# Routed attention and mixture of experts in one kernel: sums two pairs back and similarities moved to the head of a pair, routing a pair later

## The chip, the cores and the metric

The kernel runs on one core of a Trainium2 chip. The core has a matmul engine (PE, with its weight loads shown as PEld), a vector engine (DVE), a scalar engine for activations and copies (ACT), a general engine (POOL) and an engine that issues transfers (SP). [...] they wait for each other by semaphores. The metric is the device time of one execution in microseconds (us); less is better.

## The reference

Two blocks follow each other. The first is attention with routing: every query and every key is assigned to the nearest of 16 centroids of its head, and a query attends only to keys of its own cluster. The second sends every row of the result, 3072 rows of 512 numbers, to one of eight experts. Cut to what matters:

```python
# q, k, v: (4, 8, 768, 64); centroids: (8, 16, 64)
q_assign = argmax(einsum('bhsd,hcd->bhsc', q_n, c_n), -1)   # normalised
k_assign = argmax(einsum('bhsd,hcd->bhsc', k_n, c_n), -1)
mask = q_assign[..., :, None] == k_assign[..., None, :]
scores = where(mask, q @ k.T / 8, -1e9)
attn = softmax(scores)
x = (attn @ v).transpose(0, 2, 1, 3).reshape(3072, 512)

logits = x @ w_gate                     # (3072, 8)
e = argmax(logits, 1)
gate_w = softmax(logits)[row, e]
y[row] = gate_w * (relu(x[row] @ w1[e]) @ w2[e])
```

## The kernel before, in words

**Pairs.** There are 4 sequences (`B`) of 8 heads. The attention works on two heads at a time; the loop over `n` runs over 16 such pairs, four to a sequence (`HP` is 4). A pair has two halves `h` of 384 queries each, and six blocks `j` of 128 keys. For each of the 12 combinations `score` (L426 to L433) puts the products of keys and queries into a score tile `sps` and adds a mask product of 16-bit one-hot rows, `mk` and `mq`, to it; ACT then takes the exponential into a tile `A` (L445). There are three score tiles and twelve `A` tiles. From the second block of a half on, `add_up` (L451, DVE) adds the `A` tiles into `acc`. After all 12, `attend` (L457) multiplies the values by the `A` tiles, first for half 0, then for half 1, and ACT copies each finished half into `oT` (L464).

**What hangs around this stream.** Each step is a small function, placed by hand at a slot (`at_pair(n, u, f)`): `between(n, u)` runs the list of slot `u` of pair `n` in the order in which it was filled. Slots 0 to 5 lie behind the six scores of half 0 and their adds, 6 to 11 behind those of half 1, 12 behind the attention outputs of half 0, and 13 at the end of the pair.

- *For the next pair.* `prepare(n, step)`: step 0 (`turn`, L277) transposes the queries and keys just loaded; step 1 (`similar`, L291) multiplies them by the centroids on PE into a bank `mps`; steps 2 and 3 (`assign0`, `assign1`, `assign2`, L302 to L327) find on DVE each row's cluster and end with the one-hot transpose `ohT`; steps 4 and 5 (`place`, L337 and L340) copy it on ACT into `mk` and `mq`, in eight operations, keys first.
- *For the pair before.* `sum_up` (L480) sums the columns of `acc` on PE and multiplies `oT` by the gate weights, 24 matmuls into another bank `mps`; `weights_of` (L489 to L504) takes the reciprocals of the sums and collects the logits on DVE; `rows` (L510, DVE) transposes `oT`, and `store` (L517, SP) writes it to memory in four transfers.
- *Routing of a finished sequence b.* `gate`, `gate_exp` (ACT), `gate_sum` and `choose` make the softmax weight and the choice of expert; `count` (L592, L593, two small matmuls) and `number` (L598 to L605) give each row its place in its expert's list, which six indirect transfers on POOL write (L607). `count` writes into free columns of the bank that the latest `sum_up` took.

The similarities, the sums and the two halves of the attention output share two banks of the pool `ps_m`; a new tile takes a bank whose former contents have been read. In a pair the sums come first, then the similarities, then the two halves.

**Order around the change.** `sum_up` of pair n-1 and `similar` of pair n+1 stand at slot 2, so PE does three scores, sums, similarities, and then the other nine scores. `weights_of` stands at slot 2 too, `rows` and `store` at 4, the two parts of the assignment at 5 and 7, `place` at 11, and the transposes of pair n+2 behind slot 12. The transfers of queries, keys and values of pair n+2 are issued on SP at the beginning of pair n.

**Late in the attention.** In pair 12 sequence 2 is complete. Its routing is done faster, since two first expert slots are filled from sequences 0 to 2 while pairs 13 to 15 still run: `number` in pair 13, then `rank_first` (L645 to L650), places, gathers. The expert stages follow (L968, L1069 and L1088 are their matmuls); at their start the last pair's sums and the routing of sequence 3 are done.

Of the kernel before, what the change touches and what calls it, by code (L numbers as in the profile page):

```python
# [33 lines left out]
def kernel(  # L34
# [12 lines left out]
    B, H, S, D = q.shape  # L47
# [8 lines left out]
    HP = H // 2  # L56
    NPAIR = B * HP
# [28 lines left out]
    wa = ctx.enter_context(tc.tile_pool(name="weights_a", bufs=1))  # L86
    w1s = ctx.enter_context(tc.tile_pool(name="w1_sums", bufs=1))
    xp = ctx.enter_context(tc.tile_pool(name="rows", bufs=1))
    accp = ctx.enter_context(tc.tile_pool(name="accp", bufs=3))
    otp = ctx.enter_context(tc.tile_pool(name="otp", bufs=2))  # L90
    stat = ctx.enter_context(tc.tile_pool(name="stat", bufs=2))
    rt = ctx.enter_context(tc.tile_pool(name="route", bufs=1))
# [75 lines left out]
    with tc.manual_schedule(), ExitStack() as actx:  # L168
# [12 lines left out]
        def load(n):  # L181
            b, hp = divmod(n, HP)
            for d, src, name in ((QIN, q, "q_in"), (KIN, k, "k_in")):
                t = d[n] = ld.tile([P, NI, Q4], F32, name=name)
                for r in range(4):
                    s = src[b, 2 * hp + r // 2, :, Q4 * (r % 2) : Q4 * (r % 2 + 1)]
                    nc.sync.dma_start(
                        out=t[Q4 * r : Q4 * (r + 1)].rearrange("t (j a) d -> t j a d", a=4),
                        in_=s.rearrange("(a t j) d -> t j a d", a=4, j=NQ),
                    )  # L190
            if n:
                load_v(n)

        def load_v(n):
            b, hp = divmod(n, HP)
            VIN[n] = ldv.tile([P, 2, NQ, D], F32, name="v_in")
            for a in range(2):
                nc.sync.dma_start(
                    out=VIN[n][:, a], in_=v[b, 2 * hp + a].rearrange("(p j) d -> p j d", j=NQ)
                )  # L200
# [73 lines left out]
        def turn(n, w):  # L274
            src, dst, name = ((QIN, QT, "qT"), (KIN, KT, "kT"))[w]
            dst[n] = qkt.tile([P, S], F32, name=name)
            nc.vector.transpose(dst[n], src.pop(n).rearrange("p i d -> p (i d)"))  # L277
# [9 lines left out]
        def similar(n):  # L287
            ps = ps_m.tile([P, 512], F32, name="mps")
            for g in range(4):
                t = (QT, KT)[g // 2][n]  # L290
                nc.tensor.matmul(  # L291
                    ps[Q4 * g : Q4 * (g + 1), 0:HS],
                    lhsT=cT[:, n % HP].rearrange("p a c -> p (a c)"),
                    rhs=t[:, HS * (g % 2) : HS * (g % 2 + 1)],
                    start=True, stop=True,
                )
            SIM[n] = ps

        def assign0(n, part=1):

            sim = asg.tile([P, HI, 2 * C], F32, name="sim")[:, 0 : HI // part]
            nc.vector.transpose(sim.rearrange("p i c -> p (i c)"), SIM.pop(n)[:, 0 : HS // part])  # L302
            SIM[n] = sim.rearrange("p i (a c) -> p (i a) c", c=C)

        def assign1(n, part=1):
            G = 2 * HI // part
            sim = SIM[n]
            mx = asg.tile([P, 2 * HI], F32, name="mx")[:, 0:G]
            nc.vector.tensor_reduce(mx, sim, axis=AX, op=ALU.max)
            ge = asg.tile([P, 2 * HI, C], BF16, name="ge")[:, 0:G]  # L310
            nc.vector.tensor_tensor(ge, sim, mx.unsqueeze(2).to_broadcast([P, G, C]), op=ALU.is_ge)
            SIM[n] = ge

        def assign2(n, part=1):
            G = 2 * HI // part
            ge = SIM.pop(n)
            rank = asg.tile([P, 2 * HI, C], BF16, name="rank")[:, 0:G]
            nc.vector.tensor_tensor(rank, ge, first_cb[:, None, :].to_broadcast([P, G, C]), op=ALU.mult)
            top = asg.tile([P, 2 * HI], BF16, name="top")[:, 0:G]
            nc.vector.tensor_reduce(top, rank, axis=AX, op=ALU.max)  # L320
            oh = asg.tile([P, HI, 2 * C], BF16, name="oh")[:, 0 : HI // part]
            nc.vector.tensor_tensor(
                oh.rearrange("p i (a c) -> p (i a) c", c=C), rank, top.unsqueeze(2).to_broadcast([P, G, C]),
                op=ALU.is_equal,
            )
            OH[n] = asg.tile([P, HS], BF16, name="ohT")[:, 0 : HS // part]
            nc.vector.transpose(OH[n], oh.rearrange("p i c -> p (i c)"))  # L327

        def place(n, w):
            t, m = OH[n], (MQ, MK)[w][n % 2]  # L330
            for h in range(2):
                for a in range(2):
                    g = 2 * w + h
                    dst = m[D * a : D * a + Q4, HS * h : HS * (h + 1)]
                    src = t[Q4 * g : Q4 * (g + 1), :]
                    if w == 0:
                        nc.scalar.copy(dst, src)  # L337
                    else:
                        big, less = (t[Q4 * g : Q4 * (g + 1), a : a + 1] for t in (ksc2, kscn2))
                        nc.scalar.activation(dst, src, AF.Identity, bias=less, scale=big)  # L340
            if w == 0:
                OH.pop(n)
# [95 lines left out]
        def score(n, h, j):  # L438

            if n + h or j > 2:  # L440
                score_half(n, h, j, True)
            score_half(n, h, j, False)
            ps = SP.pop((n, h, j))
            A[n, h, j] = ap.tile([P, 2, HS], F32, name="A")
            nc.scalar.activation(A[n, h, j], ps[:, :, 0:HS], AF.Exp, scale=D**-0.5)  # L445

        def add_up(n, h, j):
            if j == 1:
                ACC[n, h] = accp.tile([P, 2, HS], F32, name="acc")
            first = A[n, h, 0] if j == 1 else ACC[n, h]  # L450
            nc.vector.tensor_tensor(ACC[n, h], first, A[n, h, j], op=ALU.add)  # L451
# [70 lines left out]
        def prepare(n, step):  # L522
            if not 0 <= n < NPAIR:
                return
            if step == 0:
                turn(n, 0)
                turn(n, 1)
            elif step == 1:
                similar(n)
            elif step == 2:  # L530
                assign0(n)
                assign1(n)
            elif step == 3:
                assign2(n)
            elif step == 4:
                place(n, 1)
            else:
                place(n, 0)
# [285 lines left out]
        def at_pair(n, u, f, *a):  # L824
            AT.setdefault((n, u), []).append(lambda: f(*a))

        for n in range(NPAIR):
            if n:
                at_pair(n, 2, sum_up, n - 1)
                at_pair(n, 4, rows, n - 1)  # L830
                at_pair(n, 4, store, n - 1)
            for u, step in ((2 if n else 6, 1), (5 if n else 7, 2), (7 if n else 8, 3), (11, 4), (11, 5)):
                at_pair(n, u, prepare, n + 1, step)
        for b in range(B - 1):
            n = HP * (b + 1)
            last = b == B - 2
            at_pair(n, 5 if last else 10, gate, b)
            at_pair(n, 8 if last else 11, gate_exp, b)
            at_pair(n + (not last), 9 if last else 3, gate_sum, b)
            at_pair(n + (not last), 10 if last else 9, choose, b)  # L840
            at_pair(n + 2 - last, 2, count, b)
            at_pair(n + 2 - last, 3 if last else 6, number, b)
        for n in range(1, NPAIR):
            at_pair(n, 2, weights_of, n - 1)
        n = HP * (B - 1)
        slots = range(len(EARLY))
        at_pair(n + 1, 4, rank_first)
# [20 lines left out]
        def between(n, u):  # L868
            for f in AT.pop((n, u), ()):
                f()  # L870
# [4 lines left out]
        for n in range(NPAIR):  # L875
            if n + 2 < NPAIR:
                load(n + 2)
            for h in range(2):
                for j in range(NQ):
                    score(n, h, j)  # L880
                    if j:
                        add_up(n, h, j)
                    between(n, h * NQ + j)
            for h in range(2):
                for j in range(NQ):
                    attend(n, h, j)
                if h == 0:
                    between(n, 12)
                    prepare(n + 2, 0)
            between(n, 13)  # L890
        assert not AT

# [1 line left out]
    with tc.manual_schedule(), ExitStack() as ectx:  # L894
# [262 lines left out]
        n = NPAIR  # L1157
        last = NS - 1
# [9 lines left out]
        for s in range(NS):  # L1168
# [26 lines left out]
            if s < last:  # L1195
# [16 lines left out]
                if s == 0:  # L1212
                    when = ((h2, 1), (h2, 2), (h2, 5), (h2, 6), (h2, 7), (h2, 7))
                elif s == 1:
                    when = ((h1, 9), (h1, 12), (h2, 2), (h2, 3), (h2, 6), (h2, 6))
                else:
                    when = ((h1, 9), (h1, 10), (h2, 1), (h2, 2), (h2, 2), (h2, 5))
# [297 lines left out]
```

## Time and profile before

| | |
|---|---|
| runs of the kernel | 660.87 us median of 3 (659.3 to 662.08) |
| the profiled execution | 659.27 us |
| its span in the profile | 657.5 us |
| PE busy | 644.2 us (98%) |
| DVE busy | 490.0 us (75%) |
| ACT busy | 338.8 us (52%) |
| POOL busy | 130.8 us (20%) |
| attention pairs 1 to 15 | 31.8 to 329.5 us of the span |
| exponentials L445, each | 814 ns, 192 of them |
| adds L451, each | 948 ns, 128 of them |
| copies of outputs L464, each | 481 ns, 32 of them |
| ACT waiting for `ohT` before `place` | 39.7 us in 15 waits |

The span runs from the first to the last instruction of the profile; 1.8 us of the execution lie around it. Busy time of PE is modelled for the ends of its matmuls, so the starts of its instructions are read for its rhythm, not the sum of its busy time. A line such as `150.39 0.92 PE L433 ...` in the timeline gives the start, the length, the engine, the line of the kernel and the tiles; brackets at its end give the idle time before it and what ended it. In a table of stages each row is a stretch of the span, with its length and the busy time of every engine in it, and the number of instructions in parentheses.

### The profile page before, as it was taken

To read this page: it belongs to the slowest core of one execution; us is meant where nothing else is said; L and a number is where in the kernel's file an instruction comes from. 1 tells how busy PE (TensorE), PEld (TensorE's weight loads), DVE (VectorE), ACT (ScalarE), POOL (GpSimd) and SP (SyncE) were. 2 spreads that over 40 slices of the span, in tenths; PEclk is the share of its full clock that TensorE was granted. 3 is DMA by queue.
4 is the path that set the end of the run, shared out by engine and by line. 5 is a ranking of instruction groups with operands and counts; after the bars stand their busy time and mean duration, and the time that the engine had idled before them with its cause. 6 is when DMAs were issued, how large, how long until landed. Compare 5 with 4: busy or idle time off the path is not lost.

```text
span 657.5 us, 11491 instructions
## 1 busy us (share of the span) xinstructions
PE 644.2 (98%) x4252; PEld 423.3 (64%) x4252; DVE 490.0 (75%) x845; ACT 338.8 (52%) x584; POOL 130.8 (20%) x166
## 2 busy tenths in 40 slices
PE   8999999999999999999999999999999999999996
PEld 4444544455444454544484979989797987869773
DVE  6988888998889988989887997888869365572300
ACT  4677878768878777867532333333231331323210
POOL 4500000022000300041103522324240422140010
PEclk9999999999999999999999999999999999999999
DMA  7663455443355433347475587776684835614010
GB/s 150 150 120 68 76 94 97 72 80 68 73 97 98 74 76 72 72 132 227 117 273 156 187 314 264 252 275 211 249 307 170 273 138 165 233 74 173 7 49 19
DMA packets 189760, 95.38 MB, mean 145 GB/s; under 512 B 152895, under 2 KB 171839, under 8 KB 188416
## 3 DMA queue, kind: packets, MB, share of 16 engines
q1 hardware_dynamic: 184624, 81.56, 45.2%
q0 software_dynamic: 4928, 12.97, 6.1%
q8 instruction: 35, 0.57, 0.4%
q14 instruction: 29, 0.24, 0.1%
q10 hardware_dynamic: 144, 0.03, 0.0%
HBM read 74.10 MB, written 20.70 MB: 144 GB/s over the span
## 4 chain that ended last, share of the span: by engine, by line
PE 80%; issue 10%; DVE 5%; POOL 2%; ACT 1%; DMA 1%; POOLq 0%; DVEq 0%; ACTq 0%
PE sps L433 20%; PE mps L457 16%; PE bank L968 10%; PE sbank L968 8%; PE bank L1069 7%; PE bank L1088 7%; PE sbank L1069 6%; PE mps L480 2%; PE mps L291 1%; PE bank L937 1%; DMA xg<-x_rows,gi 1%; DVE xT L780 1%; POOL tokens_of L607 1%; DVE acc L451 1%; DVE a L789 1%
## 5 line engine op out<-in xcount | busy, mean ns | idle before, releaser
L445 ACT ACTIVATE A<-sps 128x768 f32<-128x768 f32 x192 | 152.1, 814 | 30.0 <-PE sps L433 29.4
L433 PE MATMUL sps<-qT,kT 64*128 64x384 f32 x768 | 158.9, 492 | 0.0
L451 DVE TENSOR_TENSOR acc<-acc,A 128x768 f32<-128x768 f32 x128 | 121.4, 948 | 11.4 <-ACT A L445 2.9
L457 PE MATMUL mps<-A,v_in 128*64 128x384 f32 x768 | 127.4, 488 | 0.0
L433 PEld LDWEIGHTS sps<-qT,kT 64*128 64x128 f32 x768 | 66.8, 187 | 52.2 <-issue 48.4
L457 PEld LDWEIGHTS mps<-A,v_in 128*64 128x64 f32 x768 | 53.7, 137 | 70.6 <-issue 62.9
L1043 POOL DMA_INDIRECT out_dram<-z,si x30 | 47.7, 1590 | 196.0 <-DVE z L926 167.2
L607 POOL DMA_INDIRECT tokens_of<-tg,pos_i x24 | 27.5, 1147 | 270.5 <-DVE pos_i L605 264.4
L433 PE MATMUL sps<-mq,mk 64*128 64x384 bf16 x384 | 64.9, 323 | 3.1 <-ACT mq L337 1.3
L1088 PE MATMUL bank<-w,h 128*128 128x512 f32 (+2 forms) x224 | 64.4, 596 | 0.0
L340 ACT ACTIVATE mk<-ohT,kscn,ksc 32x384 bf16<-32x384 bf16 x60 | 42.0, 700 | 40.5 <-DVE ohT L327 39.7
L968 PE MATMUL bank<-xT,w 128*128 128x144 f32 (+4 forms) x288 | 47.7, 309 | 0.0
L738 POOL DMA_INDIRECT xg<-x_rows,gi x30 | 38.4, 1280 | 47.0 <-DVE si L729 16.4
L968 PE MATMUL sbank<-xc,a 128*128 128x144 f32 (+4 forms) x288 | 47.7, 309 | 0.0
L1088 PEld LDWEIGHTS bank<-w,h 128*128 128x128 f32 (+2 forms) x224 | 24.6, 151 | 32.5 <-issue 32.3
L968 PEld LDWEIGHTS bank<-xT,w 128*128 128x128 f32 x288 | 43.8, 190 | 2.6 <-issue 2.2
L451 DVE TENSOR_TENSOR acc<-A 128x768 f32<-128x768 f32 x32 | 30.4, 952 | 19.2 <-ACT A L445 19.1
L968 PEld LDWEIGHTS sbank<-xc,a 128*128 128x128 f32 x288 | 43.4, 190 | 0.0
L926 DVE TENSOR_TENSOR h<-sbank,p 128x288 f32<-128x288 f32 (+4 forms) x18 | 9.2, 514 | 45.7 <-PE sbank L968 45.5
L433 PEld LDWEIGHTS <-mk 64*128 64x128 bf16 x384 | 19.9, 94 | 29.0 <-DVE mk L383 2.6
L986 ACT ACTIVATE h<-h 128x288 f32<-128x288 f32 (+4 forms) x36 | 17.6, 488 | 38.1 <-DVE h L926 38.1
L755 DVE TENSOR_TENSOR xw<-xg,sf 128x256 f32<-128x256 f32 (+2 forms) x60 | 32.8, 606 | 0.9 <-DMA xg<-x_rows,gi 0.6
(216 smaller groups left out, 900.5 us busy)
## 6 DMA issues: line engine op xcount, KB each, us to landing
w<-in_moe_w_dram SPq DMA_DIRECT2D x20, 2048.0 KB, 10.7
v_in<-in_v_dram SPq DMA_DIRECT2D x32, 192.0 KB, 2.5
x_rows<-x SPq DMA_DIRECT2D x64, 96.0 KB, 2.4
turn_rows<-xw SPq DMA_DIRECT2D x23, 256.0 KB, 2.0
q_in<-in_q_dram SPq DMA_DIRECT2D x60, 96.0 KB, 3.2
k_in<-in_k_dram SPq DMA_DIRECT2D x60, 96.0 KB, 3.2
xs<-turn_rows SPq DMA_DIRECT2D x16, 144.0 KB, 2.8
xs<-turn_rows SPq DMA_DIRECT2D x8, 208.0 KB, 4.2
```

Source lines behind the costliest of these rows:

```text
L340: nc.scalar.activation(dst, src, AF.Identity, bias=less, scale=big)
L433: nc.tensor.matmul(SP[n, h, j][:, a, 0:HS], lhsT=kt[rows, j * P : (j + 1) * P], rhs=qt[rows, h * HS : (h + 1) * HS], start=first, stop=not ...
L445: nc.scalar.activation(A[n, h, j], ps[:, :, 0:HS], AF.Exp, scale=D**-0.5)
L451: nc.vector.tensor_tensor(ACC[n, h], first, A[n, h, j], op=ALU.add)
L457: nc.tensor.matmul(O[n, h][D * a : D * (a + 1), 0:HS], lhsT=VIN[n][:, a, j, :], rhs=A[n, h, j][:, a, :], start=(j == 0), stop=(j == NQ - 1),)
L607: ins = nc.gpsimd.indirect_dma_start(out=t_d[:, :], out_offset=bass.IndirectOffsetOnAxis(ap=pos_i[:, i : i + 1], axis=0), in_=tg[:, b, i, ...
L738: nc.gpsimd.indirect_dma_start(out=xg[0:m], out_offset=None, in_=x_d[0:rows_in, :], in_offset=bass.IndirectOffsetOnAxis(ap=g["gi"][0:m, j ...
L755: nc.vector.tensor_tensor(xw[0:m, :, :, d2 * a : d2 * (a + 1)], xg[0:m].rearrange("p (r a d b) -> p a r b d", r=HP, a=2, b=DB)[:, a], g["s ...
L968: nc.tensor.matmul(ps[:, f * T2 : (f + 1) * T2], lhsT=w[:, k, (2 * j + f) * P : (2 * j + f + 1) * P], rhs=x[:, k, :], start=first and f + ...
L1043: ins = nc.gpsimd.indirect_dma_start(out=out[:, :], out_offset=bass.IndirectOffsetOnAxis(ap=GR[s]["si"][0:rows, j : j + 1], axis=0), in_=z ...
L1069: nc.tensor.matmul(ps[:, 0:H], lhsT=x[:, k, :], rhs=y[:, k, :], start=first and k == 0, stop=k == 3, skip_group_check=not first,)
L1088: nc.tensor.matmul(ps[i * m : (i + 1) * m, :], lhsT=h[:, f, j * P : j * P + m], rhs=w[:, f, :], start=(k == 0), stop=(k == FB // n - 1),)
```

## The change

Up to pair 11 the sums of a pair are made two pairs later instead of one, at a new slot -1 ahead of the first score, and the similarities of the next pair stand beside them:

- for pairs 2 to 12 slot -1 runs `sum_up(n-2)`, slot 0 `weights_of(n-2)`, slot 3 `rows` and `store` of pair n-2 (in pair 12 these at slot 0);
- from pair 12 on `sum_up(n-1)` stays at slot 2, and `weights_of` goes to slot 3, `rows` and `store` to 5 in pair 12 and stay at 4 after it; pair 12 so has the sums of pairs 10 and 11;
- for pairs 2 to 11 `similar` goes to slot -1, the assignment to slots 2 and 4, and the transposes of pair n+2 from behind slot 12 to slot 9; elsewhere they stay;
- the routing of sequences 0 and 1 is one pair later: `gate` at slot 10 of pair 4b+5, `gate_exp` at slot 13, and so on; that of sequence 2 stays;
- `acc` has four buffers instead of three.

```diff
-    accp = ctx.enter_context(tc.tile_pool(name="accp", bufs=3))
+    accp = ctx.enter_context(tc.tile_pool(name="accp", bufs=4))
...
+        LATE = HP * (B - 1)
+
+        def pair_end(n, u, v, m):
+            at_pair(n, u, sum_up, m)
+            at_pair(n, u + 1, weights_of, m)
+            at_pair(n, v, rows, m)
+            at_pair(n, v, store, m)
+
         for n in range(NPAIR):
-            if n:
-                at_pair(n, 2, sum_up, n - 1)
-                at_pair(n, 4, rows, n - 1)
-                at_pair(n, 4, store, n - 1)
-            for u, step in ((2 if n else 6, 1), (5 if n else 7, 2), (7 if n else 8, 3), (11, 4), (11, 5)):
-                at_pair(n, u, prepare, n + 1, step)
+            if n >= 2 and n <= LATE:
+                pair_end(n, -1, 3 if n < LATE else 0, n - 2)
+            if n >= LATE:
+                pair_end(n, 2, 5 if n == LATE else 4, n - 1)
+            if n == 0:
+                steps = (6, 7, 8, 11, 11, 12)
+            elif n == 1 or n >= LATE:
+                steps = (2, 5, 7, 11, 11, 12)
+            else:
+                steps = (-1, 2, 4, 11, 11, 9)
+            for step, u in enumerate(steps):
+                at_pair(n, u, prepare, n + 1 + (step == 5), (step + 1) % 6)
         for b in range(B - 1):
             n = HP * (b + 1)
             last = b == B - 2
-            at_pair(n, 5 if last else 10, gate, b)
-            at_pair(n, 8 if last else 11, gate_exp, b)
-            at_pair(n + (not last), 9 if last else 3, gate_sum, b)
-            at_pair(n + (not last), 10 if last else 9, choose, b)
-            at_pair(n + 2 - last, 2, count, b)
-            at_pair(n + 2 - last, 3 if last else 6, number, b)
-        for n in range(1, NPAIR):
-            at_pair(n, 2, weights_of, n - 1)
+            if last:
+                when = ((n, 5), (n, 8), (n, 9), (n, 10), (n + 1, 2), (n + 1, 3))
+            else:
+                when = ((n + 1, 10), (n + 1, 13), (n + 2, 3), (n + 2, 9), (n + 3, 2), (n + 3, 6))
+            for (m, u), f in zip(when, (gate, gate_exp, gate_sum, choose, count, number)):
+                at_pair(m, u, f, b)
...
         for n in range(NPAIR):
             if n + 2 < NPAIR:
                 load(n + 2)
+            between(n, -1)
             for h in range(2):
...
                 if h == 0:
                     between(n, 12)
-                    prepare(n + 2, 0)
             between(n, 13)
```

## The prediction

> **What bounds the kernel now.** I read the page first (TensorE 98% busy, chain of waits 80% PE), then stage by stage. Below, busy time by stage, one row for each pair of heads: the stretch, its length, then busy time by engine.
>
> ```profile
> core 0: us, PE busy (x) PEld busy (x) DVE busy (x) ACT busy (x) POOL busy (x), PEclk, DMA share, GB/s
> 31.80:51.55 19.75, 19.75 (x154) 9.66 (x153) 16.68 (x25) 15.93 (x25) 0.00 (x0) 1.00 0.71 122
> 130.51:150.39 19.88, 19.88 (x157) 9.78 (x155) 18.30 (x32) 14.55 (x22) 5.28 (x5) 1.00 0.43 79
> 150.39:170.13 19.74, 19.74 (x155) 9.66 (x153) 17.36 (x27) 15.77 (x25) 1.98 (x2) 1.00 0.43 79
> 249.22:268.96 19.74, 19.74 (x154) 9.68 (x152) 16.95 (x35) 14.94 (x23) 0.00 (x0) 1.00 0.47 86
> 268.96:288.84 19.88, 19.88 (x156) 9.77 (x154) 18.21 (x45) 11.90 (x18) 6.77 (x6) 1.00 0.21 45
> 288.84:310.37 21.53, 20.21 (x154) 9.89 (x152) 19.49 (x37) 17.47 (x27) 4.58 (x4) 1.00 0.76 254
> ```
>
> A pair takes 19.74 us, or 19.88 where `count` falls into it (pairs 6, 10, 13), and PE is busy through all of it; DVE has 1.6 to 3.1 us free, ACT 3.8 or more. Only pair 14 is longer: 21.53 us, 1.3 of it idle. The chain of waits has the same rhythm:
>
> ```profile
> 43.73 7.89 PE mps L457 x48
> 51.62 2.62 PE sps L433 x18
> 54.24 1.11 PE mps L480 x24
> 56.00 7.47 PE sps L433 x54
> ```
>
> Three scores 2.62, sums 1.11, similarities 0.65 (what is left to 56.00), nine scores 7.47, attention outputs 7.89: 19.74. So up to pair 13 a pair costs what PE's own stream costs, and a moved step earns only what it changes in that stream. The timeline of PE shows what that can be (start, length):
>
> ```profile
> 150.39 0.92 PE L433 MATMUL sps<-qT,kT 64*128 64x384 f32 x4
> ...
> 151.30 0.81 PE L433 MATMUL sps<-qT,kT 64*128 64x384 f32 x4
> ...
> 152.11 0.81 PE L433 MATMUL sps<-qT,kT 64*128 64x384 f32 x4
> ...
> 153.01 0.86 PE L480 MATMUL mps<-acc,ones_s 128*32 128x192 f32 x16
> ...
> 154.01 0.49 PE L291 MATMUL mps<-qT,cT 128*32 128x384 f32 x2
> ...
> 154.77 0.92 PE L433 MATMUL sps<-qT,kT 64*128 64x384 f32 x4
> ...
> 155.68 0.81 PE L433 MATMUL sps<-qT,kT 64*128 64x384 f32 x4
> ```
>
> A score follows a score after 0.81 us (0.807 on average). It takes 0.91 (150.39 to 151.30) as the first after the outputs, 0.90 as the last before the sums, 0.91 after the similarities (154.77 to 155.68), and 0.90 before the outputs. Each change of matmul kind costs about 0.1. The outputs alone, 24 times 0.3225 (start to start of their weight loads), are 7.74, so 7.89 holds 0.05 of their start and 0.10 at their end. The same 7.89 lies between the last outputs (321.58) and the full-width matmul after them (329.47), so that 0.10 isn't the scores' doing.
>
> The one stall, and the work around a head on ACT:
>
> ```profile
> 290.86 0.32 PE L433 MATMUL sps<-mq,mk 64*128 64x384 bf16 x1 [1.10 <-ACT mq L337]
> 291.39 0.32 PE L433 MATMUL sps<-mq,mk 64*128 64x384 bf16 x1 [0.21 <-ACT mq L337]
> ```
> ```profile
> 151.54 0.86 ACT L464 COPY oT<-mps 128x384 f32<-128x384 f32 x2
> 152.28 2.24 ACT L445 ACTIVATE A<-sps 128x768 f32<-128x768 f32 x3
> 155.94 7.21 ACT L445 ACTIVATE A<-sps 128x768 f32<-128x768 f32 x9 [1.43 <-PE sps L433]
> 165.52 2.85 ACT L340 ACTIVATE mk<-ohT,kscn,ksc 32x384 bf16<-32x384 bf16 x4 [2.36 <-DVE ohT L327]
> ```
>
> The mask matmul of pair 14 needs the fifth and sixth of eight `place` operations. `place` waits for the one-hot transpose `ohT` on DVE, and the copies of the outputs (L464) stand behind `place` on ACT: in pair 6 they run from 151.54 to 152.40, up to 2.0 us after the head of pair 7 at 150.39.
>
> [...] 0.1 us at each change (scores 64x128, outputs 128x64, sums 128x32). [...] the L464 copy of pair 6's first half ran at 151.54, right behind `place`, though its matmuls ended near 146.5. [...]
>
> **The change part by part.** H is the start of a pair's first PE work; ends that I don't show are sums of the spacings named.
>
> 1. *Sums and similarities at the head, pairs 2 to 11.* Before: outputs, scores, sums, scores, outputs. After: outputs, sums, scores, outputs. The 0.10 of the first score at the head goes and the 0.09 of the third before the sums goes; the 0.10 behind the outputs stays, as it did before the full-width matmul. That is 0.20 a pair, 19.54 instead of 19.74; times 10 = 2.0 us. Outputs to sums isn't in the trace of before. If it costs nothing, 0.30 a pair (3.0 in all); if the sums pay a further 0.1 at their start, 0.10 (1.0). I take 0.20, since every change that is seen costs 0.1.
>
> 2. *Sums moved between pairs.* Pair 1 has no sums: similarities alone take 0.78 (18.90 to 19.68) instead of 1.76, so -0.98. Pair 12 has two: +1.11, as sums without similarities in pair 15 take (313.00 to 314.11). Sum +0.13.
>
> 3. *`count` of sequences 0 and 1.* It lay behind the similarities for 0.14 (19.88-19.74). Now it stands alone between two scores: 0.09 into it, 0.14 itself, 0.10 out of it, 0.33. Twice +0.19 = +0.38. It writes free columns of the sums' bank, which `number` reads at slot 6, after the outputs have started. In pair 6 of before the outputs began at 142.50 while `number` still read that bank (L599, 142.59 to 142.76), so the first outputs get the other bank; `number` at about H+14.2 is ahead of the second half at H+15.5. Nothing added.
>
> 4. *Does the head have its banks?* The sums need the bank of the first output half, the similarities that of the second. DVE in a steady pair: `weights_of` 1.47 from H+1.4, beside the sums and first scores. The first add waits for the second exp: scores start at H+1.76, exp 1.18 later (155.94 after 154.77), 0.80 and 0.81 for two: H+4.55. Then two adds 1.94, assign0/1 1.66, add 0.88, rows 0.90, add 0.87, assign2 2.07: `ohT` at H+12.87. The exps end at about H+12.6. `place` starts at H+13.04 (15.13 in pair 7 of before, 165.52-150.39), takes 5.0, and the first copy ends at H+18.46: 1.1 before the next head. The second copy can start 0.11 after the outputs (329.58 after 329.47) and takes 0.48; the similarities come 1.0 into the pair, slack 0.35. With `gate_sum` (0.79) ahead of `ohT` in pairs 6 and 10 the first slack is 0.3. So no stall; this cover is the thinnest of the change. Masks have 5 us more room than before.
>
> 5. *The rest of DVE.* After `ohT`: six adds, the turn of pair n+2 (1.79, now slot 9): end about H+20.3, the next `weights_of` is due at H+20.9. `choose` (1.37) or `number` (1.12) push it at most into time that DVE spent waiting for ACT (1.54 at 153.85). `gate_exp`, now behind the last copy, stands where ACT is idle. Zero. SP: loads of pair n+2 are issued ahead of the stores of n-2, whose four issues take 2.7 us, loads 5.5; the turn comes at H+16.6, and the load's landing is 3.2. Zero. The fourth `acc` buffer only keeps pair n-2 alive.
>
> 6. *Pairs 12 to 14.* `weights_of` goes from slot 2 to 3. In pair 12 it filled a gap in which DVE waited for the exp behind the sums (wait to 255.62); there DVE now waits and does the 1.47 later. `weights_of` and `rows` of pair 10 run at the head and fit ahead of the first add (H+1.9 to 4.3). `ohT` for pair 13 comes 1.47 later against its deadline. The sixth `place` ended at 268.56 of the 269.87 at which the second score of pair 13 was due: slack 1.3, hence a stall of about 0.3 (with semaphores). ACT and DVE enter pair 13 later: its first add at 4.66 instead of 3.08 behind the head; the waits of 0.43 and 0.21 that DVE had there shrink, so `ohT` is at 19.5 instead of 18.36 (287.32-268.96). Less the 0.3 already paid, the stall at pair 14 grows by 0.85. Together +1.15. If the moves cost nothing here, 0; if both `weights_of` and `rows` (2.4) and more land on the path, 2.5. Pair 14 has 0.9 of slack for its 0.35.
>
> Sum: -2.0 + 0.13 + 0.38 + 1.15 = -0.3 us. The profiled execution took 659.27 (span 657.5 and 1.8 around it): 658.9. The median of the runs is 1.6 higher, 660.87; on it the forecast is 660.5. With the ends of the terms, PE's part is -2.5 to -0.5 and the stalls 0 to 2.5: 658.4 to 662.9.
>
> **The rivals.**
> *A, slower: the head waits for ACT.* Were `place` to start later than about H+14.1, the first copy would end behind the next head and PE would stand at the sums in each of 11 heads. If `ohT` is 1.6 us later than I have it (half of what pair 6 of before lags behind, 16.2 against 13.0), that is 0.55 a head, 6 us: 666.5. For it: 39.7 us of ACT's waits for `ohT` before. Against: five instructions moved ahead of it.
> *B, faster: the change of kind is free and DVE's earlier turn clears pair 14.* -3.0+0.5 on PE and -1.6 for the stall: 656.8. For it: less work lies in front of pair 13. Against: `number` and `rank_first` (1.1 and 2.2 us) stay where they are.
> *C: late pairs pay the full 2.5 and PE gains the least, 1.0:* 662.9, still no change by the bound below.
>
> **How the numbers follow.** Forecast 0.55, C 0.08, A 0.20, B 0.17. About 0.5% (3.3 us) is what can be told from no change; forecast and C lie within it, B beyond it as faster, A as slower: 0.17, 0.63, 0.20. The likeliest's own range is 658.4 to 662.9; with most of B and the nearer part of A, 656.5 to 666.
>
> **What would show it.** A period of 19.54 in pairs 2 to 11 on the chain of waits, sums straight behind the outputs with no idle time; `place` about 13 us after the head; 0.33 at `count`; pair 13's first masks late by 0.3 and pair 14's stall near 2.2 instead of 1.3. I am wrong if PE idles at the heads on ACT's L464 copies (A), if the period is 19.4 and pair 14 has no stall (B), or if the expert stages change at all, since nothing in them does.

## The result, and the profile after

| | before | after |
|---|---|---|
| runs, median | 661.02 us of 6 (659.3 to 662.08) | 663.89 us of 6 (663.05 to 665.47) |
| ratio, 95% interval | | 1.0056 [1.0042, 1.007] |
| the profiled execution | 659.27 us | 663.5 us |
| its span | 657.5 us | 661.7 us |
| attention pairs 1 to 15 | 31.81 to 329.47 us | 31.59 to 333.06 us |

The kernel is 0.56% slower, where 660.5 us and no change were forecast. In the profiled executions 4.23 us were lost: 3.59 until the last pair ends, about 0.6 behind it, where the expert stages are. From the end of the last pair to the end of the span it is 327.1 to 331.3 us over all profiles of this study, and 328.1 and 329.9 in the two of the unchanged kernel, so this 0.6 can't be told from the spread.

Busy time by stage, pairs 3, 8, 12, 13 and 14 of after (stretch, length, then busy time by engine):

```profile
core 0: us, PE busy (x) PEld busy (x) DVE busy (x) ACT busy (x) POOL busy (x), PEclk, DMA share, GB/s
70.98:90.52 19.54, 19.54 (x154) 9.71 (x152) 16.55 (x26) 15.37 (x22) 0.00 (x0) 1.00 0.45 83
...
169.02:190.25 21.23, 19.81 (x155) 9.68 (x153) 17.04 (x26) 14.99 (x22) 3.07 (x4) 1.00 0.39 70
249.20:270.13 20.93, 20.93 (x179) 10.55 (x177) 17.99 (x37) 12.33 (x18) 3.21 (x3) 1.00 0.41 77
270.13:291.34 21.21, 21.00 (x156) 10.06 (x155) 18.74 (x49) 12.78 (x20) 6.46 (x6) 1.00 0.31 60
291.34:313.96 22.62, 20.21 (x154) 9.87 (x152) 20.30 (x37) 18.21 (x28) 4.58 (x4) 1.00 0.75 242
```

A common pair takes 19.54 us instead of 19.74, as forecast, and 19.88 with a `count` in it (pairs 7 and 11). But pair 8, which has nothing of its own, takes 21.23, and pairs 12 to 14 take 20.93, 21.21 and 22.62 against 19.74, 19.88 and 21.53. The chain of waits (start, length) shows pair 3, a common one, and pair 8:

```profile
71.06 1.11 PE mps L480 x24
72.81 9.89 PE sps L433 x72
...
169.09 1.11 PE mps L480 x24
170.85 3.17 PE sps L433 x18
174.89 7.54 PE sps L433 x54
```

Sums stand behind the outputs, then all twelve scores run in one piece (9.89 from 72.81). In pair 8 that piece is broken: behind the first three scores PE waits until 174.89. Before this change no pair but the 14th had idle time on PE; now the timeline of PE has these lines with idle time in brackets between 31.6 and 333 us, besides two of 0.21:

```profile
51.45 0.86 PE L480 MATMUL mps<-acc,ones_s 128*32 128x192 f32 x16 [0.67 <-ACT oT L464]
```
```profile
174.89 0.92 PE L433 MATMUL sps<-qT,kT 64*128 64x384 f32 x4 [1.42 <-ACT A L445]
```
```profile
294.45 0.32 PE L433 MATMUL sps<-mq,mk 64*128 64x384 bf16 x1 [2.19 <-ACT mq L337]
```

The first is the head of pair 2, waiting 0.67 us for a copy of the outputs. The second is pair 8: the fourth score waits 1.42 us for the exponential that has to free its bank. The third is the stall of pair 14, 2.19 us instead of 1.10. Why the exponential of pair 8 is late shows on ACT and POOL:

```profile
174.02 2.22 ACT L445 ACTIVATE A<-sps 128x768 f32<-128x768 f32 x3 [4.41 <-PE sps L433]
```
```profile
170.75 0.97 POOL L607 DMA_INDIRECT tokens_of<-tg,pos_i  x1 [0.30 <-issue]
172.03 0.97 POOL L607 DMA_INDIRECT tokens_of<-tg,pos_i  x1 [0.30 <-issue]
```

ACT is idle for 4.41 us. The first score of pair 8 is done at about 172, as its start at 170.78 says, but ACT starts at 174.02, and the events of PE's semaphore in the trace say the same: the end of the sums at 170.20 is signalled at 172.39, and the similarities and the three scores together between 173.87 and 174.09. In pair 3 each of these signals comes within 0.1 us of its end. All the while POOL issues the last of sequence 0's six scatters to `tokens_of` (the first at 164.33), which the change moved from the end of pair 6 and the head of pair 7 to the end of pair 7 and the head of pair 8, where the sums now stand.

Pair 13 is longer too. Its similarities of pair 14, on PE's timeline:

```profile
274.33 0.82 PE L291 MATMUL mps<-qT,cT 128*32 128x384 f32 x4
...
275.85 0.18 PE L592 MATMUL mps<-last,lt_b 128*128 128x8 bf16 x1
```

They take 1.52 us (274.33 to 275.85) where they take 0.76 in a common pair (154.01 to 154.77 in before), as they wait for the transposes of pair 14 on VectorE (the second ran from 274.08 to 275.02). Of pair 13's +1.33, 0.76 lie here, and 0.57 in its first three scores (3.20 until the sums instead of 2.63), which wait for their masks.

### The profile page after: what moved, and what is told of

Read it like the earlier page. It is cut to its first block, busy times and chain, and to the rows that moved or that the text cites. A ratio compares the mean times of both kernels' runs of the same rounds, so it can differ in the third digit from the quotient of the medians.

```text
span 661.7 us, 11503 instructions
## 1 busy us (share of the span) xinstructions
PE 644.9 (97%) x4252; PEld 424.5 (64%) x4252; DVE 489.4 (74%) x845; ACT 340.4 (51%) x584; POOL 132.0 (20%) x166
## 4 chain that ended last, share of the span: by engine, by line
PE 73%; DVE 17%; ACT 4%; DMA 2%; issue 2%; SPq 0%; DVEq 0%; POOL 0%; POOLq 0%; ACTq 0%
PE sps L433 16%; PE mps L457 12%; PE bank L982 11%; PE sbank L982 8%; PE bank L1083 7%; PE bank L1102 7%; PE sbank L1083 6%; DVE acc L451 5%; PE mps L480 2%; DVE a L789 2%; ACT mk L340 2%; PE mps L291 1%; PE bank L951 1%; DVE xT L780 1%; DMA turn_rows<-xw 1%
## 5 line engine op out<-in xcount | busy, mean ns | idle before, releaser
L738 POOL DMA_INDIRECT xg<-x_rows,gi x30 | 40.0, 1333 | 47.0 <-DVE si L729 16.3
```

The costliest lines, as they stand in the source:

```text
L738: nc.gpsimd.indirect_dma_start(out=xg[0:m], out_offset=None, in_=x_d[0:rows_in, :], in_offset=bass.IndirectOffsetOnAxis(ap=g["gi"][0:m, j ...
```

## The experiments

Theory S, formed from this profile: the scatters over the sums at a head make PE's signals late. Its first rival R: the stall of pair 8 is chance. Pair lengths are from head to head on PE. Where a ratio is given, both kernels were timed on the same chip; a time without a ratio is a single run. The runs of this section come from three chips: e11 and e12 from chip 1, e15 from chip 9, the others from chip 10. For before and after the chip isn't recorded.

**Is pair 8 chance?** Both kernels once more, with nothing changed.

e0_before_again: 

> The kernel before, profiled once more. Every theory: 19.74 us a pair, no idle time of PE in pairs 2 to 13, a stall of 1.1 to 1.3 us in pair 14. If its signals from PE are late in some pair by 2 us too, then the late signals seen in pairs 8 and 12 of the changed kernel are nothing that the change brings.

e1_after_again: 

> The changed kernel, profiled once more. Theory S (the sums at the head meet the scatters of number): the exp of pair 8 starts 2 us late again, and the weights_of of pairs 8 and 12 start about 2 us late again, since the six indirect transfers lie over the same head. Theory R (a random disturbance of that one execution): pairs 8 and 12 run undisturbed, 19.54 and 20.85 us, and the span is 1.5 us shorter. Both: 0.7 us of idle PE at the head of pair 2, 2.2 in pair 14.

Before again: every pair within 0.01 us of its earlier length, 661.27 us. After again: pair 8 21.49, stall 1.68; pairs 12 and 13 21.14 and 21.74; head of pair 2 0.67; 668.21 us. So the losses belong to the kernel. New in it was pair 14: 24.24 us with the same stall of 2.19 (see the last section).

Before again has late signals as well, which by its expectation means that the change doesn't bring them. In pair 13 the six scatters of sequence 2 run over the end of the first half of the outputs, and that end is signalled 2.24 us late. In pair 7, with scatters over a head of scores, one score is signalled 0.96 us late. The first costs nothing, since ACT is waiting for one-hots then; the second has ACT wait for 0.21 us, and the pair stays at 19.74. So what the change can have brought is a place where something waits for such a signal.

The signal in pair 13 tells the profiles apart: it is 1.95 to 3.50 us late in after and in all ten profiles from chip 10, and comes within 0.03 us in before, e11, e12 and e15. In these four no signal of an attention pair is late at all. Whether the chip makes the difference or the occasion isn't known.

**Move count and numbering of sequences 0 and 1, with the scatters.**

```diff
-((n + 3, 2), (n + 3, 6))   # count, number
+((n + 3, 0), (n + 3, 1))   # e2_number_early
+((n + 4 - b, 2), (n + 4 - b, 6))   # e3_number_later: sequence 0 a pair later
```

> The changed kernel with count and number of sequences 0 and 1 at slots 0 and 1 of the same pair instead of 2 and 6, so that the six scatters end about 4 us ahead of the next head. Theory S: no late signals at the heads of pairs 8 and 12, pair 8 takes 19.54 us instead of 21.2; about 1.5 us less than the changed kernel. Theory R: no steady gain, within 0.5 us of the changed kernel.

> The changed kernel with count and number of sequence 0 one pair later (pair 8 instead of 7), sequence 1 as it was. Theory S: the late start of exp and weights_of goes from the head of pair 8 to that of pair 9; pair 12 keeps its own. A theory that the place itself (pair 8) is at fault, whatever POOL does: it stays in pair 8. Theory R: neither.

e2: pairs 8 and 12 take 19.54 and 20.85, no late signal; 662.56 us, ratio 1.0028 [1.0016, 1.004]. The cost of the move was a new wait that I hadn't expected: `count` at slot 0 writes the bank that `weights_of` still reads, so pairs 7 and 11 take 20.48. e3: pair 8 has 19.88 and the loss is now in pair 9, 21.35 with a stall of 1.54; 665.39 us. The loss goes with the numbering. Whether with its scatters or its other work is the next question.

**The scatters alone.**

> The kernel after the change, with nothing moved but the six scatters of the first sequence: count and the numbering on VectorE stay in pair 7, the scatters go to slot 3 of pair 8. Theory S (the scatters on POOL, over the sums at the head, hold up PE's signals): pair 8 falls from 21.2 to about 19.5 us, its stall of 1.4 to 1.7 us before the outputs is gone, and the sums' end is signalled within 0.2 us; about 662 us. Rival D (count's matmuls or the numbering's VectorE work in pair 7 are what holds pair 8 up): pair 8 stays at 21.2 with the stall. Pairs 12 to 14 as in after.

This run tested nothing. POOL didn't hold to the slot: with nothing else in its queue it issued the scatters as soon as the places were there, at 164.13 us (164.33 in after), and pair 8 took 21.29. The test needs the instruction that they wait for to move:

```diff
             nc.vector.reduce_sum(pos, pr.rearrange("p e t -> p t e"), axis=AX)
+            POS[b] = pos
+            if b:
+                scatter(b)
+
+        def scatter(b):
+            pos = POS.pop(b)
             pos_i = rt.tile([P, TC], I32, name="pos_i")
...
+        at_pair(8, 3, scatter, 0)
```

> The kernel after the change, with the last step of the first sequence's numbering (the 0.17 us that makes the places whole numbers, which the scatters wait for) at slot 3 of pair 8 together with its six scatters; count's matmuls and all other work of the numbering stay in pair 7. So the scatters themselves start after the head of pair 8. Theory S (scatters over the sums): sums and similarities of pair 8 are signalled on time, no stall in pair 8, 19.54 us, about 1.7 us less than after. Rival D (count's matmuls or the numbering's work on VectorE in pair 7): pair 8 still 21.2 with the stall of 1.4 to 1.7 us. Pair 9: 19.54 if the scatters end before its head.

Pairs 8 and 9 take 19.54 each. On POOL the scatters start 10 us behind the head (168.19), and ACT's exponentials of pair 8 start 2.93 behind it and run in one piece:

```profile
178.58 1.67 POOL L615 DMA_INDIRECT tokens_of<-tg,pos_i  x1 [152.80 <-DVE pos_i L613]
```
```profile
171.12 9.63 ACT L445 ACTIVATE A<-sps 128x768 f32<-128x768 f32 x12 [2.34 <-PE sps L433]
```

That is what S forecast, but it doesn't settle the question. In pair 12 this kernel is as after, with the scatters of sequence 1 on the sums at its head (from 4.67 us before the head in both), and there no signal was late either. ACT in pair 12 of after, then of e12:

```profile
253.50 2.21 ACT L445 ACTIVATE A<-sps 128x768 f32<-128x768 f32 x3 [3.70 <-PE sps L433]
```
```profile
248.97 2.43 ACT L445 ACTIVATE A<-sps 128x768 f32<-128x768 f32 x3 [1.69 <-PE sps L433]
```

The exponentials start 4.30 us behind the head in after, 2.29 in e12. This is one of the profiles without late signals, so its pair 8 would probably have been on time with the scatters where they were. The runs from chip 10 have to decide. In e2, e8 and e14 (the latter two below) `count`, numbering and scatters of sequence 0 were moved, and pair 8 takes 19.54 with no late signal, in e8 and e14 with scatters that end 0.85 and 0.87 us ahead of its head. The next run leaves `count` where it was.

**Does the kernel before do it too?**

```diff
-at_pair(n + 2 - last, 3 if last else 6, number, b)
+at_pair(n + 2 - last, 3 if last else 9, number, b)
```

> The kernel before the change, with the numbering of the first two sequences at slot 9 instead of slot 6 of its pair, so that the scatters run over the sums at slot 2 of the next pair (153.0 to 153.9 us in before). Theory S1 (scatters over the sums and similarities, wherever these stand): the sums' end is signalled some 2 us late there too, the exponentials behind it start late, and pair 7 (and pair 11) takes 20.5 to 21.5 us instead of 19.74 and 19.88. Rival S2 (only at a head, where the scores that follow have no exponential in hand): the signals may come late but pair 7 stays at 19.7 to 19.9; rival S3 (nothing to do with the sums): no late signal.

The sums of pair 7 end at 155.56 and are signalled at 158.03; those of pair 11 are 2.31 us late. Pairs 7 and 11 take 20.33 and 20.58 instead of 19.74 each (the 19.88 of the expectation is pair 10's, which has the `count`). ACT in pair 7:

```profile
158.28 4.41 ACT L445 ACTIVATE A<-sps 128x768 f32<-128x768 f32 x6 [2.93 <-PE sps L433]
```

So S1 in kind, 0.6 and 0.8 in size, pair 7 less than I expected (and pairs 6 and 10 take 21.15, since the outputs wait 1.05 us for the bank that the later numbering reads, which I hadn't expected). The delay is there with the kernel before too, and `count`, which stayed at slot 2, isn't its cause. In before again two scatters also run over the head of pair 7, where only scores stand, and it costs nothing (19.74): a loss by late signals was seen only with scatters over sums, and with work behind them that waited.

No run from chip 10 parts the scatters from the numbering's work on VectorE that they follow. For the scatters speaks the time: that work is over when the first of them starts, 8 to 9 us before the last ends, and in all thirteen cases of late sums the last signal of the burst comes 0.5 to 1.5 us behind the end of the last scatter. That is an argument, not a test.

**Pairs 12 to 14: the doubled pair?** The lag taken up in pair 10 (`LATE = 10`); then with the scatters early and pair 1's assignment at slots 3 and 4; then in pair 9 with the transposes of outputs behind the assignment.

```diff
-        LATE = HP * (B - 1)
+        LATE = 10    # e7, e8; 9 in e11
...
-((n + 3, 2), (n + 3, 6))
+((n + 3, 2 - (not b)), (n + 3, 2 if b == 0 else 6))    # e8, e11
...
+            elif n == 1:
+                steps = (2, 3, 4, 11, 11, 12)    # e8, e11
...
-pair_end(n, -1, 3 if n < LATE else 0, n - 2)
+pair_end(n, -1, 3 if n < LATE else 8, n - 2)    # e11
-pair_end(n, 2, 5 if n == LATE else 4, n - 1)
+pair_end(n, 2, 10 if n == LATE else 4, n - 1)    # e11
```

> The kernel after the change, with the pair that takes up the lag (two pairs' sums) moved from pair 12 to pair 10; pairs 10 to 15 then stand as in the kernel before. Theory L (pairs 12 to 14 pay for the lag because the doubled work falls beside the routing and the last masks): pair 10 about 20.9 us, pair 11 19.9, pair 12 19.7, pair 13 19.9, pair 14 21.5 with a stall of 1.1 instead of 2.2 us; pair 8 keeps its 21.2; in all 2.3 us less than after, about 661.5 us, ratio to before 1.000 to 1.003. Rival (pairs 13 and 14 are long because of something the earlier pairs push back, such as transfers): pairs 13 and 14 stay at 21.2 and 22.6, and pair 10 is 1.3 us longer on top, about 664.5 to 665 us.

> As the run before it, with the count of the first sequence at slot 1 and its numbering at slot 2 of pair 7 instead of 2 and 6 (so that the scatters are over before pair 8), and with pair 1's assignment at slots 3 and 4 instead of 5 and 7. If the three causes found (scatters over the head of pair 8, the copies at the head of pair 2, the lag taken up in pair 12) are all there is: pair 1 18.8 us, pairs 2 to 6 19.54, pair 7 19.9, pairs 8 and 9 19.54, pair 10 20.9, pair 11 19.9, pair 12 19.7, pair 13 19.9, pair 14 21.5; 1.2 us less than before over the pairs, ratio to before 0.997 to 0.999. If something else of the change costs time: ratio 1.000 or above with the pair lengths as forecast, or a new stall in one of the pairs.

> As e8_all_mended, with the lag taken up in pair 9 (one pair earlier, before the second sequence's routing), and there the two transposes of outputs (0.97 us each on VectorE) put behind the assignment: pair 7's rows at slot 8, pair 8's at slot 10. Theory V (the doubled pair puts VectorE behind, so that the one-hots, which in before are done 3.9 to 5.0 us ahead of the head, come 2.7 to 2.9 us ahead of it, and the head waits for its masks in every pair until VectorE has caught up): one-hots again 3.8 us or more ahead of heads 10 to 13; pair 9 about 20.9 us, pair 10 19.7 to 20.0, pair 11 19.9 to 20.1, pair 12 19.7 to 19.9, pair 13 19.9 to 20.3, pair 14 21.5 to 22; ratio to before 0.998 to 1.000. Rival (the later pairs are longer for another reason, such as the later routing or the weights' loads): pairs 11 to 13 stay at 20.3 to 20.6 and pair 14 at 22.6, ratio 1.003 or more.

| | pair 8 | 9 | 10 | 11 | 12 | 13 | 14 | ratio to before |
|---|---|---|---|---|---|---|---|---|
| before | 19.74 | 19.74 | 19.88 | 19.74 | 19.74 | 19.88 | 21.53 | |
| after | 21.23 | 19.54 | 19.54 | 19.88 | 20.93 | 21.21 | 22.62 | 1.0056 [1.0042, 1.007] |
| e7_catch_up_10 | 21.58 | 19.54 | 20.85 | 20.43 | 20.27 | 20.63 | 22.62 | 1.0071 [1.0054, 1.0088] |
| e8_all_mended | 19.54 | 19.54 | 20.85 | 20.42 | 20.28 | 20.64 | 24.25 | 1.0036 [1.0021, 1.0051] |
| e11_spread | 19.54 | 20.85 | 21.73 | 20.23 | 20.28 | 20.64 | 22.62 | 1.0064 [1.0049, 1.008] |

All three miss in pairs 11 to 14, e11 in pair 10 too. (In the changed kernels a `count` is in pair 11, so 19.88 is its length without loss.) Wherever the doubled pair stood, it cost its 1.1 and the pairs after it were 0.3 to 1.1 too long, with the same 20.28, 20.64 and 22.62 in pairs 12, 13 and 14; the 24.25 of e8 is the same stall of 2.19 with the granted clock at 0.50 behind it (last section). Moving the transposes didn't help either: PE stood still for 0.71 us at the sums of pair 10, which took 21.73. (The head of pair 2 was free of idle time in e8 and e11, but in e2, e3 and e7 too, where pair 0 happened to have its one-hots 0.9 us or more earlier than the kernels with the wait.) A loss that stays in the late pairs wherever the doubled pair stands is hardly that pair's. What the late pairs share is `weights_of` at slot 3; before, it was at slot 2.

**The weights at slot 2.** In e13 that alone; in e14 beside the changes of e8; in e15 with the lag up to pair 12 as in the change, `count` and `number` of sequences 0 and 1 at slots 1 and 2, and pair 1's assignment as in e8.

```diff
-            at_pair(n, u + 1, weights_of, m)
+            if m == n - 2:
+                at_pair(n, u + 1, weights_of, m)
...
+        for n in range(LATE, NPAIR):
+            at_pair(n, 2, weights_of, n - 1)
```

> The kernel after the change, with the weights of the pair before back at slot 2 (as in before) instead of slot 3 in pairs 12 to 15; nothing else is moved. Theory W (at slot 2 the 1.47 us of VectorE fill its wait for the second exponential; at slot 3 they come behind a third add and push the one-hots of each of these pairs some 1.3 us nearer to the head, until the head waits for its masks): one-hots 3.9 us or more ahead of head 13 instead of 2.7; pair 12 20.8 to 20.9 us, pair 13 19.9 to 20.3 instead of 21.2, pair 14 21.5 to 21.9 with a stall of 1.1 to 1.5 us instead of 22.6 with 2.2; 1.7 to 2.2 us less than after. Rival V (the second set of sums and rows in pair 12 is what puts VectorE behind, wherever the weights stand): pairs 13 and 14 stay within 0.3 us of 21.2 and 22.6.

> As e8_all_mended (lag taken up in pair 10, scatters over before pair 8, pair 1's assignment early), with the weights back at slot 2 from pair 10 on. Theory W: pair 10 20.85 us, pair 11 19.9 to 20.1 instead of 20.4, pair 12 19.74 to 19.8 instead of 20.3, pair 13 19.88 to 20.0 instead of 20.6, pair 14 21.5 to 21.7 instead of 22.6 or more; over the pairs about 1.0 to 1.3 us less than before, ratio to before 0.997 to 0.999. Rival V: pairs 11 to 14 as in e8_all_mended, ratio 1.003 or more.

> The lag stays until pair 12 as in the change; the count of the first two sequences is at slot 1 and the numbering at slot 2 of pairs 7 and 11 (no scatter over a head with sums), the weights are back at slot 2 from pair 12 on, pair 1's assignment is at slots 3 and 4. If the late signals at the head of pair 12 are what is left of pair 13's length: pair 8 19.54 us, pair 12 20.85, pair 13 19.9 to 20.2, pair 14 21.5; the same total as e14_mended_weights within 0.5 us, ratio to before 0.997 to 0.999. If the doubled sums, beside the third sequence's routing, are: pair 13 20.6 to 21.2, pair 14 21.5 to 22, ratio 0.999 to 1.001.

| | pair 8 | 10 | 11 | 12 | 13 | 14 | ratio to before |
|---|---|---|---|---|---|---|---|
| e13_late_weights | 21.34 | 19.54 | 19.88 | 21.18 | 21.72 | 21.53 | 1.0049 [1.0032, 1.0067] |
| e14_mended_weights | 19.54 | 20.85 | 19.88 | 19.74 | 19.88 | 21.20 | 0.9976 [0.9968, 0.9985] |
| e15_mended_12 | 19.54 | 19.54 | 19.88 | 20.85 | 19.88 | 21.22 | 0.9958 [0.9944, 0.9973] |

e14 differs from e8 in the weights alone, both on chip 10: pairs 11 to 13 are at 19.88, 19.74 and 19.88, with no loss left, and pair 14 at 21.20, a little below the forecast. In e13 pair 14 is back at 21.53, but pair 13 stayed long, which I hadn't forecast. What the slot does is seen on VectorE, pair 14, in after and then in e13:

```profile
298.32 0.96 DVE L451 TENSOR_TENSOR acc<-A 128x768 f32<-128x768 f32 x1 [1.00 <-ACT A L445]
...
300.62 0.96 DVE L451 TENSOR_TENSOR acc<-acc,A 128x768 f32<-128x768 f32 x1 [0.28 <-ACT A L445]
301.50 0.38 DVE L489 STREAM_TRANSPOSE slt<-mps 128x192 f32<-128x192 f32 x1
```
```profile
297.39 0.96 DVE L451 TENSOR_TENSOR acc<-A 128x768 f32<-128x768 f32 x1 [1.00 <-ACT A L445]
...
299.33 0.38 DVE L489 STREAM_TRANSPOSE slt<-mps 128x192 f32<-128x192 f32 x1
```

With slot 3 a third add comes first, which has to wait for its exponential, and the transpose `slt` starts 3.18 us behind the first add instead of 1.94. What such a delay of 1.24 in pair 13 does to the masks of pair 14 shows in the one-hots that pair 13 makes for it, in after and in e13:

```profile
290.41 0.58 DVE L327 STREAM_TRANSPOSE ohT<-oh 128x384 bf16<-128x384 bf16 x1
```
```profile
289.48 0.58 DVE L327 STREAM_TRANSPOSE ohT<-oh 128x384 bf16<-128x384 bf16 x1
```

They end 0.36 us ahead of the head of pair 14 in after (291.34) and 1.45 in e13 (291.51), and the stall is 2.19 in the one and 1.09 in the other.

Pair 13 is 21.72 in e13 and 19.88 in e15, which has the same doubled pair 12, but no late signal at its head. So the doubled pair isn't what makes pair 13 long; it is the late signals (in e13 the sums of pair 12 were signalled 3.18 us late), at 1.84 us, although PE hardly stood still in pair 12. They hold up ACT and VectorE at pair 12's head, and these pass it on: the one-hots for pair 13 end 2.15 us ahead of its head in e13, 4.20 in e15. (e15 comes from another chip; from chip 10 alone, with slot 3, pair 13 is 20.83 in e2, without late signals in pair 12, and 21.20 to 21.74 in e1, e3 and e9, with them.) Slot 3 alone costs pair 13 0.95 (20.83 in e2 and e12). The two don't add up: both together are 1.3 to 1.9.

e15 is faster than the kernel before by 0.4%, 656.88 us against 659.83 on its chip, a little more than forecast; its pairs come to 0.2 us less than e14's. Its stages, pairs 8, 12, 13 and 14, with the columns of the first table:

```profile
168.27:187.81 19.54, 19.54 (x154) 9.71 (x152) 17.20 (x27) 15.38 (x22) 0.00 (x0) 1.00 0.49 87
246.77:267.62 20.85, 20.85 (x178) 10.34 (x176) 19.40 (x41) 14.04 (x21) 0.00 (x0) 1.00 0.53 96
267.62:287.50 19.88, 19.88 (x157) 9.78 (x155) 18.60 (x45) 12.67 (x19) 6.46 (x6) 1.00 0.28 54
287.50:308.72 21.22, 20.22 (x155) 9.87 (x153) 19.18 (x37) 17.17 (x26) 4.58 (x4) 1.00 0.78 258
```

## Why the prediction was wrong, by its steps

The sum of -0.3 us fails at three places: step 5 put at nothing what cost 1.7 in pair 8, step 6 has the pairs 13 and 14 too short by 1.3, and step 4 overlooked what took back pair 1's gain of 1.1. The rest was right to 0.1 but for the start of pair 1, which came 0.22 earlier. In us, by pair:

| | ahead of pair 1 | pair 1 | 2 to 11 | 12 | 13 | 14 | sum |
|---|---|---|---|---|---|---|---|
| forecast | 0 | -0.98 | -1.62 | +1.11 | +0.3 | +0.85 | -0.3 |
| measured | -0.22 | +0.12 | +0.08 | +1.19 | +1.33 | +1.09 | +3.59 |

Pairs 2 to 11 gained 1.6 as forecast, and pair 8 gave it back.

- *Step 1, -2.0: right in kind and size.* Every pair from 2 to 11 without another loss takes 19.54. The trace of before gave the price of a change of matmul kind, 0.1 (a score beside one takes 0.90 to 0.91, one between scores 0.81). Two such costs less are the 0.20 that was gained; the rivals of 19.44 and 19.64 fell. Why a change costs 0.1 wasn't shown.
- *Step 2: right in its own terms.* Pair 1's sums are worth -0.97 (18.76 or 18.77 in seven profiles), the doubled pair +1.11 (20.85).
- *Step 3: right.* 0.34 at each `count`. What I wrote of its bank matters at other slots: e2's 0.55 us wait.
- *Step 4: right for the steady pairs, wrong in pair 1.* One-hots came 12.94 us behind the head (forecast 12.87), and no steady head waited for the copies. But pair 1 keeps the late assignment, slots 5 and 7, and has the new head after it; there PE waited 0.29 to 0.67 for the first copy in five of the profiles, and 0.34 more of pair 1's 19.86 lie in its own first three scores, whose masks were late. I had made the sum for a steady pair alone and then taken -0.98 for pair 1. With the assignment at slots 3 and 4 the wait is gone: in e8, e11 and e15 pair 1's one-hots end 7.4 us ahead of the head of pair 2. In e9, e12 and e13, which start alike (pair 0's one-hots 3.6 us ahead), they end 5.6 us ahead, and PE waits 0.29.
- *Step 5, "zero": the step that failed most.* It follows VectorE and SP. It doesn't follow POOL: moving `number` from slot 6 of pair 4b+6 to slot 6 of pair 4b+7 moves six scatters that run for 9 us over a head as before, but that head now has sums. Cost: 1.7 in pair 8 (21.23 against 19.54), and 0.1 to 0.3 in pair 12 with up to 1.8 in pair 13. Nothing in the trace of before showed the price: no scatter lay on sums there, and the outputs of pair 13, which had scatters on them, were signalled on time, though 2.24 us late when the same kernel ran again. That the overlap was new could be read from it.
- *Step 6, +1.15: right mechanism, mis-sized.* `weights_of` at slot 3 was named with its 1.47 (in pair 14 it came 1.24 later in after than in e13), and pair 14's +0.85 measured 1.09 (stall 2.19, forecast near 2.2). Pair 13's +0.3 measured 1.33: its masks were late as forecast, by more (0.57), and the similarities of pair 14 also wait on VectorE (0.76), a wait that I didn't look for. In the 0.57 the late signals of pair 12 have a part: in e2, without them, it is 0.21, and pair 13 takes 20.83, +0.95.
- *The rivals.* A (heads wait for copies) has the right sign and size on another mechanism: it is seen at one head of eleven. C's 662.9 took only the late pairs.

What stays open is why the signals are late, and why not in every execution. Scatters lay on sums in fourteen pairs of eight profiles, and thirteen times the sums were signalled 2.2 to 3.9 us late; pair 12 of e12 is the exception, in a profile that has no late signal anywhere. In the attention, signals late by some 2 us or more were seen only under scatters, on sums or on outputs. No path on which scatters and PE's signals meet was shown.

## What to carry to other kernels

When a step is moved, follow every queue that it issues to, POOL's with its length in time, and ask what the other engines do where it will now run; in e9_scatters_later POOL issued the scatters at 164.13 us, 4.68 ahead of the head of pair 8, although they were written at slot 3 of that pair. An operation that fills its engine's wait for another is worth its place: `weights_of`, one slot later, stood behind that wait, 1.24 us later, and pair 13 took 0.95 more. Before a trace is taken to show that a change removes a delay, see that the delay occurs elsewhere in that trace: e12 had none to remove. A steady period doesn't cover the first and the last rounds: they have other slots, as pair 1 and pairs 12 to 14 have here.

## What the runs showed of the hardware

PE's signals came late while the starts of PE's own instructions showed nothing: sums 2.2 to 3.9 us and outputs 1.95 to 3.50 us late under indirect scatters, behind sums with the next signals in a burst. In the trace it looks as if ACT waited for a score that had long been done (pair 8 of after: done at about 172, ACT's start at 174.02). All ten profiles from chip 10 and after have it, three from chips 1 and 9 and before don't.

The stall of 2.2 us cost about 1.6 more than itself in four of the eight profiles that have it. In e1_after_again the stall of pair 14 ends at 295.30, and 1.6 us later the granted clock (third column from the end, between the busy times and the DMA share) halves:

```profile
296.00:297.00 1.00, 1.00 (x9) 0.73 (x10) 1.00 (x2) 0.96 (x3) 0.00 (x0) 0.97 0.56 131
...
298.00:299.00 1.00, 1.00 (x12) 0.40 (x12) 0.18 (x2) 1.00 (x3) 0.92 (x1) 0.50 0.84 360
...
300.00:301.00 1.00, 1.00 (x16) 0.33 (x8) 0.90 (x2) 0.00 (x0) 0.96 (x1) 0.83 1.15 492
```

It stays at 0.50 from 296.94 to 300.34, as the shares of the first and the last of these rows give, 3.4 us, and costs about 1.6 (24.24 against 22.62). Of the eight profiles with this stall at 2.2 us, four show it (pair 14 at 24.2 to 24.3) and four don't; the seven with a stall of 1.84 or less never do. Why the clock halves in four of these eight and not in the others wasn't shown. That no stall of 1.84 us or less did it is seven profiles, not a threshold.
